# A decode attention and gMLP kernel: two rows a partition of w_out come through two GpSimd gathers instead of SyncE's queue

## The chip, the core and the metric

The kernel runs on one core of a Trainium2 chip. The metric is the device time of one execution in microseconds (us). The core has five engines that run their own instruction streams: PE (matmul, with PEld for its weight loads), DVE (vector), ACT (scalar), POOL (GpSimd) and SP (SyncE, which here only issues transfers). Sixteen DMA engines move data between HBM and the on-chip SBUF, which has 128 partitions. Transfers issued by one engine stand in a queue of their own.

## What is computed

One decode step for one token `x` of 576 values: a normalised `xn` feeds a windowed attention (32 query heads, 16 key/value heads, the last 4096 positions of the caches) and a gated MLP, and both are added to `x`. Cut to what matters:

```python
xn = layernorm(x)
# attention: W = 4096, Dh = 128, each key/value head serves two query heads
q = (xn @ wq).reshape(32, 128)
p = softmax(q @ k[:, -W:].T * 128 ** -0.5)
A = (p @ v[:, -W:]).reshape(1, 4096) @ wo            # wo: 4096 x 576
# gMLP with one token, Fh = 2304
z = gelu(xn @ w_in)                                  # w_in: 576 x 4608
g = w_sp * layernorm(z[2304:]) + b_sp
B = (z[:2304] * g) @ w_out                           # w_out: 2304 x 576
out = x + A + B
```

Some 51 MB of weights and caches are read for it, and almost nothing is written.

## The kernel before

**The stream of loads.** SP issues 17 loads, and each begins once its slot in SBUF is free. In order: wq in two parts (`rest` in slot "d", the remainder in "a"), K[0] ("b"), K[1] ("c"), w_in in two parts (seven pieces in "a", two in `rest`), K[2] ("b"), V[0] ("c"), K[3] ("d"), V[1] ("a"), V[2] ("b"), V[3] ("c"), then w_out (all NF = 18 rows a partition, L106) and wo in five pieces of 14, 9, 6, 2 and 1 rows a partition (L108 and L109). Every load covers all 128 partitions. A row of w_out or wo in one partition is 576 values of two bytes, 1152 B. Partition p of w_out holds rows 18p to 18p + 17.

**The work.** Keys come in four groups g of four heads, each group in two halves c. `keys(g, c)` transposes half a group on DVE (L258), `scores(g, c)` multiplies it with the query on PE (L265), `sm_a(g)` takes the maximum on DVE (L286 and the small steps of `spread`) and the exponentials on ACT (L292), `sm_b(g)` transposes the probabilities on DVE (L303, tile `pt`) and rearranges them on ACT (L306), `sums(g)` and `pv(g)` multiply by ones and by V on PE (L312, L329), and `tail(g)` normalises on DVE (L339, L343), turns the result by small matmuls (L350) and writes 32 partitions of `Y` (L357). The gated MLP is woven in: `z_mms` (L365), `z_exp`, `z_gelu` and `z_norm`, which ends in `hv` (128 x 18). In `z_norm` POOL does one instruction, a power (L404), between two groups of DVE's.

**The order** is written out by hand (lines 420 to 477); each engine does its instructions in the order of the program. Small results in PSUM share one buffer, the pool `ps_m` with tag "m", and `pt` is a single buffer of the pool `single`.

**The end.** `out_mms` (L463) adds one row of w_out or wo a partition to the two output accumulators: two matmuls, one over 264 and one over 312 columns, which stand in different column groups of PE and run side by side. `hv` rows 0 to 11 come first, then `tail(3)`, then `hv` rows 12 to 17, then the 32 rows of wo with `Y` as the weights, in the order of their loads. After the last, DVE and ACT copy the accumulators out (L480, L481), and ACT stores them (L482).

Of the kernel before, what the change touches and what calls it, by code (L numbers as in the profile page):

```python
# [7 lines left out]

FP32 = mybir.dt.float32
BF16 = mybir.dt.bfloat16  # L10
ALU = mybir.AluOpType
ACT = mybir.ActivationFunctionType
AXX = mybir.AxisListType.X

D = 576
# [12 lines left out]
NF = FH // 128  # L28
CUT = (0, 264, D)
XP = D // 3  # L30
EPS = 1e-5
SCALE = DH ** -0.5
GELU_C = 0.7978845608028654
# [4 lines left out]
def kernel(  # L38
# [21 lines left out]
    work = ctx.enter_context(tc.tile_pool(name="work", bufs=2))  # L60
    ktpool = ctx.enter_context(tc.tile_pool(name="ktpool", bufs=2))
    single = ctx.enter_context(tc.tile_pool(name="single", bufs=1))
    ps_s = ctx.enter_context(tc.tile_pool(name="ps_s", bufs=1, space=bass.MemoryType.PSUM))
    ps_o = ctx.enter_context(tc.tile_pool(name="ps_o", bufs=1, space=bass.MemoryType.PSUM))
    ps_m = ctx.enter_context(tc.tile_pool(name="ps_m", bufs=1, space=bass.MemoryType.PSUM))
# [8 lines left out]
    def rows(slot, src, name, lo, n, at=None):  # L74

        w = src.shape[1]
        if at is None:
            t = big.tile([P, n * w], BF16, name=f"{name}{lo}", tag=slot)[:]
        else:
            t = slot[:, at:at + n * w]  # L80
        v = t.rearrange("p (s c) -> p s c", c=w)
        nc.sync.dma_start(v, src.rearrange("(p s) c -> p s c", p=P)[:, lo:lo + n, :])  # L82
        return [(lo + s, v[:, s, :]) for s in range(n)]
# [19 lines left out]
    V[2] = load_kv("b", A_v_cache, 2, "v")  # L103
    V[3] = load_kv("c", A_v_cache, 3, "v")
    ends = [big.tile([P, TP * DH], BF16, name=f"end{n}", tag="ad"[n]) for n in range(2)]
    wout_sb = rows(ends[0], B_w_out, "wout", 0, NF, 0)  # L106
    wo_sb = []
    for n, t, at in ((14, 1, 0), (9, 1, 14), (6, 0, NF), (2, 0, NF + 6), (1, 0, NF + 8)):  # L108
        wo_sb += rows(ends[t], A_wo, "wo", len(wo_sb), n, at * D)  # L109
# [132 lines left out]
    for a in range(4):  # L242
        for h in range(2):
            for k2 in range(2):
                nc.vector.tensor_scalar_mul(qbv[:, a, h, k2], qpv[:, h, k2], mask4[:, a:a + 1])


    Y = const.tile([P, 32], BF16, name="Y")
    KT = {}
# [34 lines left out]
    def sm_a(g):  # L284
        s = S[g % 2]
        nc.vector.tensor_reduce(out=mx[:, 0:1], in_=s[:], op=ALU.max, axis=mybir.AxisListType.XY)  # L286
        bk = spread(mx, mb, g, ALU.max, "m")
        nm = work.tile([P, 1], FP32, name=f"nm{g}", tag="nm")
        nc.vector.tensor_scalar_mul(nm[:], bk[:, 0:1], -SCALE)  # L289
        for x in range(GK):  # L290
            lo, hi = 32 * x, 32 * x + 32
            nc.scalar.activation(pz[lo:hi, :, :, x, :], s[lo:hi].rearrange("p a (t r e) -> p (a t) r e", r=8, e=2),  # L292
                                 ACT.Exp, bias=nm[lo:hi, 0:1], scale=SCALE, accum_out=lx[lo:hi, g:g + 1])
        st[g] = {}
# [101 lines left out]
    def z_norm(G, sz):  # L396
        psz = ps_m.tile([P, 512], FP32, name="psz", tag="m")
        nc.tensor.matmul(psz[:, 0:2], lhsT=ones_f[:], rhs=sz[:], start=True, stop=True)
        mz = const.tile([P, 4], FP32, name="mz")
        nc.vector.tensor_scalar_mul(mz[:, 0:2], psz[:, 0:2], 1.0 / FH)  # L400
        nc.vector.tensor_mul(mz[:, 2:3], mz[:, 0:1], mz[:, 0:1])
        nc.vector.tensor_sub(mz[:, 2:3], mz[:, 1:2], mz[:, 2:3])
        nc.vector.tensor_scalar_add(mz[:, 2:3], mz[:, 2:3], EPS)  # L403
        nc.gpsimd.tensor_tensor(out=mz[:, 3:4], in0=mz[:, 2:3], in1=mhalf[:], op=ALU.pow)  # L404
        zn = const.tile([P, NF], FP32, name="zn")
        nc.vector.tensor_scalar(out=zn[:], in0=G[:, 1], scalar1=mz[:, 0:1], scalar2=mz[:, 3:4],
                                op0=ALU.subtract, op1=ALU.mult)
        nc.vector.tensor_scalar(out=zn[:], in0=zn[:], scalar1=wb[:, 0:1], scalar2=wb[:, 1:2],
                                op0=ALU.mult, op1=ALU.add)
        hv = const.tile([P, NF], BF16, name="hv")  # L410
        nc.vector.tensor_mul(hv[:], G[:, 0], zn[:])
        return hv
# [7 lines left out]
    for g in range(2):  # L420
        for c in range(2):
            keys(g, c)
            scores(g, c)
            if g == 1 and c == 0:
                sm_a(0)
    zps = z_mms()
    sm_b(0)
    sm_a(1)
# [24 lines left out]
    tail(1)  # L453
    sm_a(3)
    hv = z_norm(G, sz)
    sums(2)
    pv(2)
    tail(2)
    sm_b(3)
    sums(3)  # L460
    pv(3)

# [12 lines left out]
    out_hv(2)  # L475
    for t, wv in wo_sb:
        out_mms(Y, t, wv, t == 31)

    res = const.tile([1, D], BF16, name="res")
    nc.vector.tensor_copy(res[:, 0:CUT[1]], acc[0])  # L480
# [32 lines left out]
```

## Time and profile before

| What | Before |
|---|---|
| median of 3 runs | 126.97 us (126.78 to 127.12) |
| the profiled execution | 126.89 us |
| its span, first to last instruction | 125.1 us |
| HBM read over the span | 50.96 MB, 407 GB/s |
| busy: PE, DVE, ACT, POOL | 70.8, 78.5, 43.2, 7.1 us |

The lines cited are those of the kernel before. The profile has a record for every instruction and for every DMA packet; busy times do not count waiting. The chain of waits starts at the last instruction and goes back, at each step, to what released it. The view of stretches gives, for chosen windows of time, the busy time of each engine and the mean busy share of the 16 DMA engines. The granted clock of PE is a share of its full speed, 1.0 or 0.5.

### The profile page before, as it was taken

The page shows a single profiled execution, that of the slowest core. Times are in us where ns is not written, and L with a number is a line of the kernel's source. Part 1 is how long each engine was busy: PE and PEld are TensorE (multiplying, and loading weights), DVE is VectorE, ACT ScalarE, POOL GpSimd, SP SyncE. Part 2 cuts the span into 40 slices and gives each one's busy share as a digit, 9 for nine tenths or more (in the row PEclk, how much of TensorE's full clock was granted, in tenths as well). Part 3 has the DMA queues.
Part 4 walks back from the last instruction along what each step waited for, and adds up shares of the span by engine and source line. Part 5 has one row for each costly group of instructions (what it writes and reads, how often), then busy time and mean ns, then how long its engine had stood idle before and what let it go on. Part 6 is the DMA issues. An engine that isn't in the chain of part 4 may idle for free.

```text
span 125.1 us, 1617 instructions
## 1 busy us (share of the span) xinstructions
PE 70.8 (57%) x626; PEld 28.9 (23%) x626; DVE 78.5 (63%) x150; ACT 43.2 (34%) x101; POOL 7.1 (6%) x19
## 2 busy tenths in 40 slices
PE   0012841009878469998390992059892932049992
PEld 0001201001101013998000131002211411015850
DVE  6745025899799976308999367999938359003301
ACT  2100011000000956996069008707801941940001
POOL 2961000000000000000000000000000100000000
PEclk9999998555995867755559599657998555555899
DMA  4999899998999999898999989999999999999960
GB/s 118 511 422 440 385 471 440 398 492 356 487 420 402 385 493 461 377 492 372 461 451 398 482 367 477 401 451 430 409 482 398 451 394 440 418 413 416 428 237 0
DMA packets 2611, 51.06 MB, mean 408 GB/s; under 512 B 299, under 2 KB 428, under 8 KB 684
## 3 DMA queue, kind: packets, MB, share of 16 engines
q1 hardware_dynamic: 2592, 50.96, 95.2%
q8 instruction: 5, 0.08, 0.2%
q14 instruction: 2, 0.02, 0.0%
q10 hardware_dynamic: 12, 0.00, 0.0%
HBM read 50.96 MB, written 0.00 MB: 407 GB/s over the span
## 4 chain that ended last, share of the span: by engine, by line
DMA 61%; DVE 30%; PE 5%; SPq 1%; issue 1%; ACT 0%; DVEq 0%
DMA k<-in_A_k_cache_dram 37%; DMA end<-in_A_wo_dram 25%; DVE kT L258 22%; DVE pt L303 4%; PE S L265 3%; PE acc L465 1%; SPq L82 1%; DVE mx L286 1%; DVE on L343 1%; DVE om L339 1%; PE yps L350 0%; ACT res L481 0%; DVE rs L320 0%; DVE mt L275 0%; DVE mb L281 0%
## 5 line engine op out<-in xcount | busy, mean ns | idle before, releaser
L265 PE MATMUL S<-kT,Qb 128*8 128x512 bf16 x128 | 32.5, 1148 | 23.3 <-DVE kT L258 22.8
L258 DVE STREAM_TRANSPOSE kT<-k 128x1024 f32<-128x1024 f32 x32 | 36.8, 1207 | 6.5 <-DMA k<-in_A_k_cache_dram 6.5
L292 ACT ACTIVATE pz<-S,nm 32x1024 bf16<-32x1024 f32 x16 | 19.1, 1192 | 33.6 <-DVE nm L289 20.6
L306 ACT COPY PT<-pt 32x128 f32<-32x128 f32 x64 | 19.8, 309 | 17.2 <-DVE pt L303 16.5
L329 PE MATMUL ops<-v,PT 128*32 128x512 bf16 x128 | 11.0, 505 | 6.8 <-ACT PT L306 6.8
L265 PEld LDWEIGHTS <-Qb 128*8 128x8 bf16 x128 | 3.5, 96 | 45.0 <-issue 34.8
L303 DVE STREAM_TRANSPOSE pt<-pz 128x1024 f32<-128x1024 f32 x8 | 9.4, 1210 | 0.8 <-ACT pz L292 0.8
L339 DVE SCALAR_TENSOR_TENSOR om<-ops,rs,dmask 128x512 f32<-128x512 f32 x4 | 3.0, 750 | 10.5 <-PE ops L329 10.3
L365 PEld LDWEIGHTS <-win 128*128 128x128 bf16 x126 | 7.9, 165 | 1.9 <-issue 1.9
L365 PE MATMUL zps<-XT,win 128*128 128x2 bf16 x126 | 8.0, 202 | 0.0
L286 DVE TENSOR_REDUCE mx<-S 128x1 f32<-128x1024 f32 x4 | 4.9, 1214 | 3.9 <-PE S L265 3.9
L329 PEld LDWEIGHTS <-PT 128*32 128x32 bf16 x128 | 3.7, 117 | 11.5 <-ACT PT L306 6.9
L226 ACT CAST q_rep<-qps 128x512 bf16<-128x512 f32 x2 | 1.2, 586 | 14.9 <-DVE q_rep L228 14.9
L404 POOL TENSOR_TENSOR mz<-mz,mhalf 128x1 f32<-128x1 f32 x1 | 0.6, 554 | 85.5 <-DVE mz L403 85.5
L183 PE MATMUL ps_x<-ones_b,xtw 1*128 1x1 bf16 x9 | 0.4, 162 | 8.7 <-DVE xtw L181 8.7
L465 PE MATMUL acc<-end,Y 128*1 128x312 bf16 (+1 forms) x64 | 4.9, 285 | 0.3 <-DMA end<-in_A_wo_dram 0.3
L228 DVE CAST q_rep<-qps 128x512 bf16<-128x512 f32 x2 | 1.4, 692 | 5.1 <-PE qps L217 4.5
L481 ACT CAST res<-acc 1x312 bf16<-1x312 f32 x1 | 0.4, 411 | 11.7 <-PE acc L465 11.7
L350 PE MATMUL yps<-on,sel 128*32 128x32 f32 x32 | 2.0, 210 | 4.1 <-DVE on L343 4.1
L343 DVE TENSOR_REDUCE on<-om 128x128 f32<-128x512 f32 x4 | 4.2, 1042 | 0.1
L480 DVE CAST res<-acc 1x264 bf16<-1x264 f32 x1 | 0.4, 420 | 5.2 <-PE acc L465 5.2
L465 PE MATMUL acc<-end,hv 128*1 128x264 bf16 (+1 forms) x36 | 3.6, 360 | 0.0
(92 smaller groups left out, 56.6 us busy)
## 6 DMA issues: line engine op xcount, KB each, us to landing
k<-in_A_k_cache_dram SPq DMA_DIRECT2D x4, 4096.0 KB
v<-in_A_v_cache_dram SPq DMA_DIRECT2D x4, 4096.0 KB, 26.0
win<-in_B_w_in_dram SPq DMA_DIRECT2D x1, 4032.0 KB, 27.1
wq<-in_A_wq_dram SPq DMA_DIRECT2D x1, 3584.0 KB, 12.8
end<-in_B_w_out_dram SPq DMA_DIRECT2D x1, 2592.0 KB, 22.3
end<-in_A_wo_dram SPq DMA_DIRECT2D x1, 2016.0 KB
end<-in_A_wo_dram SPq DMA_DIRECT2D x1, 1296.0 KB
rest<-in_B_w_in_dram SPq DMA_DIRECT2D x1, 1152.0 KB
```

The source lines that it names most:

```text
L258: nc.vector.transpose(dst[:, 1024 * n:1024 * (n + 1)], src[:, 1024 * n:1024 * (n + 1)])
L265: nc.tensor.matmul(S[g % 2][32 * x:32 * x + 8, c, :], lhsT=Qb[:, GK * g + x, be].rearrange("p a h -> p (a h)"), rhs=kv[:, be // 2, be % 2, x],
L286: nc.vector.tensor_reduce(out=mx[:, 0:1], in_=s[:], op=ALU.max, axis=mybir.AxisListType.XY)
L292: nc.scalar.activation(pz[lo:hi, :, :, x, :], s[lo:hi].rearrange("p a (t r e) -> p (a t) r e", r=8, e=2), ACT.Exp, bias=nm[lo:hi, 0:1], sc ...
L303: nc.vector.transpose(dst[:, 1024 * n:1024 * (n + 1)], src[:, 1024 * n:1024 * (n + 1)])
L306: nc.scalar.copy(PT4[32 * a:32 * a + 32, :, x, :], pt[32 * x:32 * x + 32, :, 2 * a:2 * a + 2])
L329: nc.tensor.matmul(ops[32 * q:32 * q + 32, :], lhsT=d["PT"][:, t0 // 2:t0 // 2 + 2].rearrange("p t x h e -> p (t x h e)"), rhs=V[g][:, t0: ...
L339: nc.vector.scalar_tensor_tensor(out=om[:].rearrange("p c d -> p (c d)"), in0=ops[:], scalar=d["rs"][:, 0:1], in1=dmask[:].rearrange("p c ...
L343: nc.vector.reduce_sum(on[:], om[:].rearrange("p c d -> p d c"), axis=AXX)
L350: nc.tensor.matmul(yps[32 * g:32 * g + 32, :], lhsT=sel[:, dq, :], rhs=d["on"][:, 32 * dq:32 * dq + 32], start=(dq == 0), stop=(dq == 3), ...
L365: nc.tensor.matmul(zps[:, :, t], lhsT=wt[:, t, :], rhs=XT[:, s, :], start=(s == 0 and t == 0), stop=(s == NS - 1 and t == NF - 1), skip_gr ...
L465: nc.tensor.matmul(acc[n], lhsT=lhs[:, col:col + 1], rhs=wv[:, CUT[n]:CUT[n + 1]], start=False, stop=last, tile_position=(0, 32 * n))
```

## The change

The last two rows a partition of w_out (rows 16 and 17 of 18; 2304 B a partition, 288 KB in all) leave SP's load, which now brings `NM` = 16 rows. They come by two gathers on POOL's own queue. Gather 0 writes partition p's own pair of rows into `ext[:, 0]`, but not for 32 "spared" partitions (20 to 27, 52 to 59, 68 to 71, 88 to 91, 100 to 103, 120 to 123). Gather 1 brings those 32 pairs into 32 other, "given" partitions (72 to 87 and 104 to 119) of `ext[:, 1]`. A partition that a gather skips has an index beyond the bound. `ext` is zeroed first, so that skipped partitions add nothing.

The indices are made on the chip: POOL writes them in a row, spreads them over a diagonal, and two PE matmuls with ones turn them into a column, which DVE copies to integers. `hv`'s last two columns are moved from the spared to the given partitions by one matmul with `move`, a permuted identity. `gap.tile` is only room left empty; `ext`, `move`, `idx` and `hx` lie behind all the buffers that were there before. `both` takes turns with `pt` in its buffer.

```diff
+NX = 2
+NM = NF - NX
+PAIRS = NF // NX
+FAR = 4096
+SPARED = ((20, 8), (52, 8), (68, 4), (88, 4), (100, 4), (120, 4))
+GIVEN = (72, 80, 104, 108, 112, 116)
...
-    wout_sb = rows(ends[0], B_w_out, "wout", 0, NF, 0)
+    wout_sb = rows(ends[0], B_w_out, "wout", 0, NM, 0)
...
+    gap.tile([P, 176], BF16, name="unused")
+    ext = far.tile([P, 2, NX, D], BF16, name="ext")
+    nc.gpsimd.memset(ext[:], 0.0)
+    move = more.tile([P, P], BF16, name="move")
+    nc.gpsimd.memset(move[:], 0.0)
+    for (lo, n), at in zip(SPARED, GIVEN):
+        nc.gpsimd.tensor_copy(move[:, at:at + n], ident[:, lo:lo + n])
+    both = single.tile([P, 4, P], FP32, name="both", tag="pt")
+    which = []
+    for g in range(2):
+        col = both[:, 2 * g].bitcast(I32)
+        if g == 0:
+            nc.gpsimd.iota(col, pattern=[[PAIRS, P]], base=PAIRS - 1, channel_multiplier=0)
+            for lo, n in SPARED:
+                nc.gpsimd.memset(col[:, lo:lo + n], FAR)
+        else:
+            nc.gpsimd.memset(col, FAR)
+            for (lo, n), at in zip(SPARED, GIVEN):
+                nc.gpsimd.iota(col[:, at:at + n], pattern=[[PAIRS, n]], base=PAIRS * lo + PAIRS - 1, channel_multiplier=0)
+        diag = both[:, 2 * g + 1]
+        nc.gpsimd.tensor_copy(diag, col)
+        nc.gpsimd.tensor_tensor(out=diag, in0=diag, in1=ident[:], op=ALU.mult)
+        which.append(diag)
+
+    def rows_to_take():
+        pick = ps_m.tile([P, 2], FP32, name="pick", tag="m")
+        for g, diag in enumerate(which):
+            nc.tensor.matmul(pick[:, g:g + 1], lhsT=diag, rhs=ones_f[:, 0:1], start=True, stop=True)
+        idx = more.tile([P, 2], I32, name="idx")
+        nc.vector.tensor_copy(idx[:], pick[:])
+        which[:] = [idx[:, g:g + 1] for g in range(2)]
+
+    def load_ext():
+        pairs = B_w_out.rearrange("(r s) c -> r (s c)", s=NX)
+        for g in range(2):
+            nc.gpsimd.indirect_dma_start(
+                out=ext[:, g].rearrange("p s c -> p (s c)"), out_offset=None, in_=pairs,
+                in_offset=bass.IndirectOffsetOnAxis(ap=which[g], axis=0),
+                bounds_check=P * PAIRS - 1, oob_is_err=False)
...
             if g == 1 and c == 0:
                 sm_a(0)
+                rows_to_take()
...
     hv = z_norm(G, sz)
+    load_ext()
     sums(2)
     pv(2)
     tail(2)
     sm_b(3)
+    hx_ps = ps_m.tile([P, 32], FP32, name="hx_ps", tag="m")
+    nc.tensor.matmul(hx_ps[:, 0:NX], lhsT=move[:], rhs=hv[:, NM:NF], start=True, stop=True)
+    hx = more.tile([P, NX], BF16, name="hx")
+    nc.vector.tensor_copy(hx[:], hx_ps[:, 0:NX])
     sums(3)
     pv(3)
...
     for t, wv in wo_sb:
         out_mms(Y, t, wv, t == 31)
+        if t == 13:
+            for j in range(NX):
+                out_mms(hv, NM + j, ext[:, 0, j, :], False)
+                out_mms(hx, j, ext[:, 1, j, :], False)
```

More of the change, by code (lines that the diff above doesn't have):

```diff
@@ L10 @@
 BF16 = mybir.dt.bfloat16
+I32 = mybir.dt.int32
 ALU = mybir.AluOpType
@@ L62 @@
     single = ctx.enter_context(tc.tile_pool(name="single", bufs=1))
+    gap = ctx.enter_context(tc.tile_pool(name="gap", bufs=1))
+    far = ctx.enter_context(tc.tile_pool(name="far", bufs=1))
+    more = ctx.enter_context(tc.tile_pool(name="more", bufs=1))
     ps_s = ctx.enter_context(tc.tile_pool(name="ps_s", bufs=1, space=bass.MemoryType.PSUM))
```

## The prediction

> **What bounds the kernel now.** I read the page first, for the load of the engines.
>
> ```profile
> span 125.1 us, 1617 instructions
> ...
> DMA  4999899998999999898999989999999999999960
> ...
> q1 hardware_dynamic: 2592, 50.96, 95.2%
> q8 instruction: 5, 0.08, 0.2%
> ```
>
> The DMA engines are full from the first slice to the 38th; no compute engine is busy over 63%. So the stream of loads sets the pace, and q8, which is no load of the program, takes five turns of 16 KB on the same engines. Then the end of the chain of waits (start us, us, what):
>
> ```profile
> 90.41 30.86 DMA end<-in_A_wo_dram
> 121.27 0.04 issue
> 121.31 1.39 PE acc L465 x17
> 122.70 0.02 issue
> 122.72 0.41 ACT res L481
> ```
>
> The wo piece of 6 rows, issued at 90.41, lands at 121.27, and PE had waited 0.28 us for it. The list of DMA issues gives the last row (issued 91.35) 31.0 us to landing: 122.35. Next the view of stretches over those last microseconds (the DMA share is the column before the last):
>
> ```profile
> 120.00:120.25 0.25, 0.25 (x8) 0.15 (x6) 0.00 (x0) 0.00 (x0) 0.00 (x0) 1.00 0.91 346
> 120.25:120.50 0.25, 0.25 (x6) 0.15 (x5) 0.00 (x0) 0.00 (x0) 0.00 (x0) 1.00 0.60 230
> 121.00:121.25 0.25, 0.03 (x1) 0.00 (x0) 0.00 (x0) 0.00 (x0) 0.00 (x0) 1.00 0.23 92
> 121.25:121.50 0.25, 0.19 (x4) 0.16 (x5) 0.00 (x0) 0.00 (x0) 0.00 (x0) 1.00 0.25 92
> 121.50:121.75 0.25, 0.25 (x8) 0.24 (x6) 0.00 (x0) 0.00 (x0) 0.00 (x0) 1.00 0.27 97
> ```
>
> A share of 0.25 is four of sixteen engines: most are done by 120.5, four work on until 121.9. The 16 KB turns would explain four: windows around 36.5, 57.2, 77.7 and 101.0 us each hold one q8 packet (0.93 to 0.96 us long), and the fifth, at 120.6, comes when most engines are done. Last, the timeline, for what stands beside these:
>
> ```profile
> 56.69 3.50 DVE L258 STREAM_TRANSPOSE kT<-k 128x1024 f32<-128x1024 f32 x3 [5.44 <-DMA k<-in_A_k_cache_dram]
> 100.80 0.75 DVE L339 SCALAR_TENSOR_TENSOR om<-ops,rs,dmask 128x512 f32<-128x512 f32 x1 [1.94 <-PE ops L329]
> 117.30 0.20 DVE L357 CAST Y<-yps 32x32 bf16<-32x32 f32 x1 [0.78 <-PE yps L350]
> 117.77 3.26 PE L465 MATMUL acc<-end,Y 128*1 128x264 bf16 x44
> 121.31 0.90 PEld L465 LDWEIGHTS <-Y 128*1 128x1 bf16 x16 [0.62 <-issue]
> 122.38 0.08 PEld L465 LDWEIGHTS <-Y 128*1 128x1 bf16 x1 [0.17 <-issue]
> ```
>
> PE can start wo only when `Y` is there (117.50), and runs almost without a pause from then on; at the end it waits for the 6-row piece (0.28) and for the last row (landed 122.35, weights at 122.38). **Two things end nearly together: the late four engines and PE's own stream of rows.** The gain is capped by the second.
>
> **The loads' end.** The late engines take the last 3 rows (each engine 8 partitions, 3 x 8 x 1152 B = 27.6 KB) between the landings at 121.27 and 122.35, 1.08 us, or 25.6 KB a us. Two rows less on each are 18.4 KB, 0.72 us: the last row lands at 121.63, the 6-row piece at 120.55. The given engines get 18.4 KB more; if they are of those done by 120.5, they end 0.72 later, about 121.2. The bytes in all stay; how a gather spreads its rows over engines no row shows. It lies between all of the 0.72 taken off the late four, nothing (rows spread evenly), and 0.72 added to one of them. I take the first.
>
> [...]
>
> **PE's stream.** Removed: hv rows 16 and 17 ahead of wo (4 matmuls). Added after wo's 14th row: 4 rows (8 matmuls). The 44 matmuls from 117.77 are 22 rows; the starts of those with 312 columns, the longer of each pair, lie 0.1325 apart. Before, that stream was still at hv when Y came, and took its first wo row at 117.82; with two rows (0.27) less ahead, it takes it at 117.56. Then 32 + 4 = 36 rows: the last starts at 117.56 + 35 x 0.1325 = 122.20, and ends 0.29 later, 122.49. Before, the last started at 122.38. So PE gains 0.18, and by its times (6-row piece at 121.14, last row at 122.20) the loads above are early enough. Had the loads not moved, PE would wait as before, and the gain were 0.
>
> **The indices.** POOL's 26 small instructions follow L200 (11.1 us). Rows: a memset of 128x4096 took 3.5 us, so ext's 128x2304 some 2.0; small copies 0.2, memsets 0.1; iotas and the mask multiply have no row, between 0.1 and 0.6 (the power). Sum 6 to 10 us, done by 22; POOL is next wanted at 97.2 and the diagonals at 42. DVE's query work beside it may lose its 0.4 us of slack before K[0] (23.63); the 5.44 us at 56.69 cover that.
>
> The wait they add: DVE's index copy stands between sm_a(0) and keys(1, 1), and needs two PE matmuls that stand behind scores(1, 0). DVE would have begun keys(1, 1) at 40.20. scores(1, 0) ends at 42.16 (38.14 + 4.02), one 128x128 f32 matmul (L312) takes 0.38 to 0.55, two 0.8 to 1.1, the copy 0.2: keys(1, 1) begins at 43.1 to 43.5, 2.9 to 3.3 late. Queued behind: scores(1, 1), sm_b(0), z_mms, sm_a(1). DVE then stands ready near 54.3 and still waits for K[2] at 56.66: 2.4 of the 5.44 are left. ACT's second exponentials end near 60.5; the transposes that want them begin at 61.2. z_mms end at 62.0 to 62.4 instead of 59.03, and SP waits for them to issue K[3] and V[1]. The queue ahead of K[3] is 26.8 MB; at 430 GB/s from 1.73 it runs dry near 64. An issue took 1.0 us to its first packet (0.73 to 1.73). Room: 0.6 to 1.0. Price 0; uncovered, the stream stops for what is missing.
>
> **The rest.** Two gathers on POOL after L404 (97.7) replace nothing on SP, whose w_out load is the same one instruction with fewer bytes; `ext` is first read at 119.4, 21 us later. hx: one matmul and one copy behind sm_b(3), before sums(3); both lie in the 4.8 us in which PE waits for ACT (pv(3) at 111.04). Price 0. Outside the span lie 126.89 - 125.1 = 1.8 us; no row bears on a change there: 0.
>
> Sum, against the profiled 126.89: -0.18, 126.71; that execution stands 0.08 under the median, so **126.79** in its terms. About 0.3% (0.38 us) can be told from no change, so this counts as none.
>
> **Rivals.**
>
> 1. *PE keeps up, the loads alone set the end.* The last 16 weight loads go in 0.90 us, 0.1125 a row. At that step 36 rows take 4.05 us from 117.55, and the end follows the landing: -0.72, 126.25. Against: the 312-column starts at 0.1325, steady over 22 rows.
>
> 2. *Other engines are late than the spared.* The 16 KB turns come one engine at a time, and no view says which; the changed program has other instructions. If none of the four is relieved, but no late one given more: 0. If a late one is among the given: it ends 0.72 later, last row at 123.07, 127.69. For the forecast speaks a match of counts alone: four are spared, four are late.
>
> 3. *The other side: the gathers hold DVE.* They start at 97.7, together with z_norm's end on DVE (L406, L408, L411, then the reciprocal for tail(2)). If POOL's descriptor work shuts DVE out, these wait, then `om` (100.80), `Y`, pt, ACT's 5.0 us, pv(3) and the last Y, one for one. Slack is the 1.94 us ahead of `om`. No row shows a gather: two lie between 2 x 0.1 and 2 x 3.5 us (POOL's shortest and longest). It is slower by over 0.3% from a hold of 2.5 us (1.94 + 0.18 + 0.38); at 3.5, one longest instruction, +1.38 gives 128.35. Against: beside pz's memset on POOL (4.71 to 8.22), DVE's memset of S took 0.91 as without.
>  [...]
>
> 4. *K[3] late.* With an issue latency of 2.5 us instead of 1.0, a hole of 0.5 to 0.9: the loads end at 122.1 to 122.5, 126.8 to 127.1.
>
> **Chances.** Forecast 0.47 (own range 126.5 to 127.1; 0.40 of it within 0.3%, 0.05 faster, 0.02 slower); rival 1 0.18 (faster); rival 2 0.16 (0.13 slower, 0.03 same); rival 3 0.13 (slower); rival 4 and what else is unseen 0.06 (0.04 slower, 0.02 same). Faster 0.23, same 0.45, slower 0.32. The range reaches from rival 1 to the worse half of rival 2, 126.2 to 127.8, and leaves out most of rival 3.
>
> **What would show it.** In the changed profile: the DMA share near the end falls from 0.9 to 0 within about 1 us, without a shelf at 0.25; PE's last 36 rows run without a wait, their first at 117.5, and end near 122.5; DVE stands about 3 us before L258 near 40 and still waits over 2 us for K[2]; no dip of the DMA share at 64; `om` for group 2 at 100.8. A shelf that is still there, or longer, is rival 2; om late, rival 3; a dip, rival 4. I am wrong if the first Y row is not at 117.5, for then the cap is not where I put it.

## The result, and the profile after

The changed kernel takes 128.12 us (median of 6 runs, 127.93 to 128.41) against 126.91 (126.78 to 127.12, 6 runs) for the kernel before: a ratio of 1.0096, 95% interval 1.008 to 1.0112. It is slower by 1.2 us, and it lies outside the range that was forecast. The profiled execution took 128.41 us with a span of 126.3; before, 126.89 and 125.1. So 1.2 us of the loss lie in the span and 0.3 outside it in that pair of executions.

Lines below are those of the changed kernel: L285 and L287 are the index matmuls and their copy, L293 the gathers, L308 the transposes of the keys, L389 `om`, L521 the output rows. First the head of its page, with its DMA row (busy share of the 16 engines in 40 slices) and its queues:

```profile
span 126.3 us, 1670 instructions
...
DMA  3999999899998999999899998989989899999940
...
q1 hardware_dynamic: 2592, 50.66, 94.0%
q0 software_dynamic: 160, 0.30, 0.6%
q8 instruction: 5, 0.08, 0.2%
```

The loads still fill the span to the 38th slice, and part of the 39th. The gathers are the 160 packets of q0, with 0.3 MB and 0.6% of the engines' time, and as many bytes less are in q1. The end of the chain of waits (start us, us, what):

```profile
90.95 32.16 DMA end<-in_A_wo_dram
123.15 0.68 PE acc L521 x6
123.85 0.41 ACT res L541
```

The chain still ends in a wo piece, but it is now the piece of 2 rows, landed at 123.11, and six matmuls of three rows follow it; before it was the piece of 6 rows, landed at 121.27, with seventeen. The timeline says which waits PE has among the last rows (the number in brackets is the idle time ahead, and what ended it):

```profile
116.26 0.20 DVE L407 CAST Y<-yps 32x32 bf16<-32x32 f32 x1 [0.53 <-PE yps L400]
...
119.42 1.36 PE L521 MATMUL acc<-end,Y 128*1 128x264 bf16 x18 [0.36 <-DMA end<-in_A_wo_dram]
...
121.47 0.96 PE L521 MATMUL acc<-end,Y 128*1 128x264 bf16 x12 [0.69 <-DMA end<-in_A_wo_dram]
...
123.15 0.66 PE L521 MATMUL acc<-end,Y 128*1 128x264 bf16 x6 [0.72 <-DMA end<-in_A_wo_dram]
```

The last part of `Y` is written 1.04 us earlier than before (117.30), and PE waits for loads three times, 1.77 us together. PE has time to spare; the loads do not come. The view of stretches (us, busy time by engine, then granted clock, DMA share, GB/s) shows how the loads end:

```profile
120.75:121.00 0.25, 0.03 (x1) 0.00 (x0) 0.00 (x0) 0.00 (x0) 0.00 (x0) 1.00 1.06 374
121.00:121.25 0.25, 0.00 (x0) 0.00 (x0) 0.00 (x0) 0.00 (x0) 0.00 (x0) 1.00 0.67 254
121.75:122.00 0.25, 0.25 (x8) 0.25 (x5) 0.00 (x0) 0.00 (x0) 0.00 (x0) 1.00 0.25 74
122.25:122.50 0.25, 0.18 (x3) 0.00 (x0) 0.00 (x0) 0.00 (x0) 0.00 (x0) 1.00 0.06 9
122.75:123.00 0.25, 0.00 (x0) 0.00 (x0) 0.00 (x0) 0.00 (x0) 0.00 (x0) 1.00 0.08 28
```

Nearly all engines work until 121.0, as the rebalancing wanted; before, the share was down to 0.6 by 120.5. The share then falls, and from 122.25 to 123.04 it is a shelf of 0.06 to 0.08. That is one engine of sixteen. The last row lands at 123.47 on it, and on the next engine at 122.52. The fifth 16 KB packet of q8 started at 120.90 and took 0.93 us.

The second thing to see is the index wait and what it moves (timeline):

```profile
42.38 0.61 PE L285 MATMUL pick<-ones_f,both 128*128 128x1 f32 x4
...
43.02 0.16 DVE L287 CAST idx<-pick 128x2 int32<-128x2 f32 x1 [2.64 <-PE pick L285]
43.09 4.62 DVE L308 STREAM_TRANSPOSE kT<-k 128x1024 f32<-128x1024 f32 x4
...
56.51 4.63 DVE L308 STREAM_TRANSPOSE kT<-k 128x1024 f32<-128x1024 f32 x4 [2.19 <-DMA k<-in_A_k_cache_dram]
...
62.14 0.54 SPq L98 DMA_DIRECT2D k<-in_A_k_cache_dram  x1
```

DVE stands 2.64 us for the index and begins `keys(1, 1)` at 43.09 instead of 40.20; it has 2.19 of its 5.44 us before K[2] left, and K[3] is issued at 62.14 instead of 59.06. Summed over all engines, the bytes moved by a given time fall behind those of before by 0.10 us at 64, 0.23 at 68, 0.50 at 102 and 0.70 at 110. The loss is not spread evenly, as the packets show below.

### The profile page after: what moved, and what is told of

It is laid out like the page before. It is cut to its first block, busy times and chain, and to the rows that moved or that the text cites. A ratio compares the mean times of both kernels' runs of the same rounds, so it can differ in the third digit from the quotient of the medians.

```text
span 126.3 us, 1670 instructions
## 1 busy us (share of the span) xinstructions
PE 70.7 (56%) x635; PEld 29.5 (23%) x635; DVE 80.4 (64%) x152; ACT 43.4 (34%) x101; POOL 14.8 (12%) x47
## 4 chain that ended last, share of the span: by engine, by line
DMA 48%; DVE 37%; PE 8%; ACT 1%; issue 1%; SPq 1%; ACTq 1%; POOL 0%; DVEq 0%
DMA end<-in_A_wo_dram 25%; DVE kT L308 21%; DMA k<-in_A_k_cache_dram 18%; DMA xrow<-in_A_x_dram 5%; DVE pt L353 4%; PE S L315 3%; PE qps L227 3%; DVE Qb L255 2%; DVE xn L212 2%; DVE q_rep L238 1%; DVE xtw L191 1%; DVE mx L336 1%; ACT q_rep L236 1%; SPq L92 1%; DVE on L393 1%
## 5 line engine op out<-in xcount | busy, mean ns | idle before, releaser
L315 PE MATMUL S<-kT,Qb 128*8 128x512 bf16 x128 | 33.0, 1162 | 21.1 <-DVE kT L308 20.6
L308 DVE STREAM_TRANSPOSE kT<-k 128x1024 f32<-128x1024 f32 x32 | 36.8, 1207 | 2.3 <-DMA k<-in_A_k_cache_dram 2.2
L379 PE MATMUL ops<-v,PT 128*32 128x512 bf16 x128 | 10.5, 487 | 4.2 <-ACT PT L356 4.2
L389 DVE SCALAR_TENSOR_TENSOR om<-ops,rs,dmask 128x512 f32<-128x512 f32 x4 | 3.0, 750 | 9.1 <-PE ops L379 8.9
L521 PE MATMUL acc<-end,Y 128*1 128x264 bf16 (+1 forms) x64 | 5.0, 285 | 1.8 <-DMA end<-in_A_wo_dram 1.8
L362 PE MATMUL lps<-lx,lsum 128*128 128x1 f32 x8 | 1.9, 304 | 4.6 <-DVE hx L515 2.5
L521 PEld LDWEIGHTS <-Y 128*1 128x1 bf16 x64 | 3.4, 83 | 3.4 <-issue 2.9
```

Source lines behind the costliest of these rows:

```text
L308: nc.vector.transpose(dst[:, 1024 * n:1024 * (n + 1)], src[:, 1024 * n:1024 * (n + 1)])
L315: nc.tensor.matmul(S[g % 2][32 * x:32 * x + 8, c, :], lhsT=Qb[:, GK * g + x, be].rearrange("p a h -> p (a h)"), rhs=kv[:, be // 2, be % 2, x],
L379: nc.tensor.matmul(ops[32 * q:32 * q + 32, :], lhsT=d["PT"][:, t0 // 2:t0 // 2 + 2].rearrange("p t x h e -> p (t x h e)"), rhs=V[g][:, t0: ...
L389: nc.vector.scalar_tensor_tensor(out=om[:].rearrange("p c d -> p (c d)"), in0=ops[:], scalar=d["rs"][:, 0:1], in1=dmask[:].rearrange("p c ...
L521: nc.tensor.matmul(acc[n], lhsT=lhs[:, col:col + 1], rhs=wv[:, CUT[n]:CUT[n + 1]], start=False, stop=last, tile_position=(0, 32 * n))
```

## The experiments

The table holds the result in short, and the sections behind it tell each step. Down to e14 each kernel has one edit more than the line above it; e17 relieves 16 partitions more and also spreads the given rows over other partitions. The difference is the ratio less one, times 126.9.

| Kernel | median us | ratio to before, 95% interval | difference us |
|---|---|---|---|
| the changed kernel | 128.12 | 1.0096, 1.008 to 1.0112 | +1.2 |
| index copy later on DVE (e1) | 127.86 | 1.0075, 1.0058 to 1.0092 | +0.95 |
| and fewer instructions on POOL (e13) | 127.71 | 1.0065, 1.0049 to 1.008 | +0.8 |
| and the pairs to other partitions (e14) | 126.88 | 1.0004, 0.9995 to 1.0013 | +0.05 |
| and 16 partitions more relieved (e17) | 126.74 | 0.9986, 0.9977 to 0.9995 | -0.2 |

### The index wait, and the gathers by themselves

Four kernels: the copy of the index moved behind `keys(1, 1)` on DVE, ahead of `z_mms` (e1); the indices but no gathers, with 18 rows of w_out from SP again (e2); one gather in which every partition gets its own pair, with no partition spared (e3); and products of w_out left out (e4, below).

```diff
 e1:
-                rows_to_take()
+                pick = rows_to_take()
+    rows_as_index(pick)
 e2:
-    wout_sb = rows(ends[0], B_w_out, "wout", 0, NM, 0)
+    wout_sb = rows(ends[0], B_w_out, "wout", 0, NF, 0)
-    load_ext()
-        for t, wv in wout_sb[6 * c:6 * c + 6]:
+        for t, wv in wout_sb[6 * c:min(6 * c + 6, NM)]:
-                out_mms(hv, NM + j, ext[:, 0, j, :], False)
+                out_mms(hv, NM + j, wout_sb[NM + j][1], False)
 e3:
-            for lo, n in SPARED:
-                nc.gpsimd.memset(col[:, lo:lo + n], FAR)
-        for g in range(2):
+        for g in range(1):
             nc.gpsimd.indirect_dma_start(
```

> The index copy on DVE moves behind keys(1, 1), so DVE no longer waits 2.64 us for PE; all else as in the changed kernel (128.1 us). Theory hole (the late issue of K[3] at 62.1 us opened a gap in the stream at 64 us and left the engines out of step, so 32 KB packets took 1230 ns instead of 1213 from 62 to 102 us): K[3] is issued near 59.1 again, packets are back at 1213 ns, the loads end 0.3 to 0.4 us earlier, 127.7 us. Theory gathers (their own packets cost the stream what it lost): no change, 128.1. Theory fetch (the fifth 16 KB instruction fetch at 120.9 us makes one loaded engine 0.95 us late): no change, 128.1.

> The changed kernel with all of its index work, but without the gathers: SP loads all 18 rows of w_out again, PE multiplies the same number of rows in the same order. Theory gathers: the stream is as before the change but for the hole, the loads end near 122.3 as before, 126.9 to 127.2 us. Theory hole: 0.35 us of the lost 0.7 stays, 127.2 to 127.5. Theory fetch: PE's program is as long as in the changed kernel, so the fifth fetch comes near 120.9; it costs 0.95 us if it falls on an engine that is still loaded (about 127.9) and nothing if the engine is done.

> One gather of all 128 partitions' own two rows, none skipped, none moved to another partition (the second half of ext stays zero and is multiplied all the same). So the gather is there and the rebalancing is not. If sparing four engines brings their 0.72 us: without it the four that served a 16 KB fetch end 1.4 us behind the rest again, and the last of them, with the fifth fetch or not, sets the end: 128.1 to 128.8 us. If the skipped indices of the second gather cost (its packets of 8 bytes): 127.9. Theory fetch alone: 128.1.

Measured: e1 127.86 (ratio 1.0075, 1.0058 to 1.0092), e2 127.83 (1.0065, 1.0044 to 1.0087), e3 127.43 (1.0039, 1.0025 to 1.0053). In e1 `keys(1, 1)` starts at 40.23 and K[3] is on time again; the bytes are 0.04 us behind at 68 and 0.15 at 110, not 0.23 and 0.70. In e2, which has no gather at all, they are 0.32 behind at 68 and 0.41 at 110, and one engine lands its last row at 123.20. So the loss of the stream comes mostly from the index wait, not from the gathers. e3 came out under all its forecasts (127.9 to 128.8).

The packets show how the wait costs. The profile does not number the engines, but a packet starts within a few ns of where the last one of its engine ends, and every engine carries the loads in the same order of sizes, so the packets can be joined into sixteen chains (worked out from the packets' records; in places where two engines end within a few ns the joining is a choice, and it is led by those sizes). Before, every engine goes over to K[3] without a pause, at 64.1 to 66.0. In e2 K[3] is issued at 61.90, and fourteen engines still go over without a pause; two stand empty for 0.8 us each, and their first packets of K[3] start at 65.39 and 66.09 and take 1.85 and 2.06 us in place of 1.21. The second of these two is the engine that lands last, and the fifth 16 KB packet is not in its chain. So e2's 127.83 lies near the 127.9 that the fifth packet was to give, but by luck. The chain of waits has its 6-row piece 0.8 us later than before:

```profile
90.40 31.68 DMA end<-in_A_wo_dram
122.07 0.04 issue
122.12 1.45 PE acc L520 x18
```

In e3 two engines stand empty, for 1.9 and 0.6 us, and the first of them lands last; and in the changed kernel one, for 0.8: it is the one that lands next to last, at 122.52. With the late copy (e1, and e5 and e6 below) none does.

Two kernels more have both edits: late copy without gathers (e5), and late copy with one plain gather (e6).

> The index work without the gathers, and with the index copy behind keys(1, 1): SP loads all 18 rows, K[3] is issued near 59.1 us. Against the run with the index work alone (127.83 us) this differs only in where DVE waits. Theory hole: all of what that run lost comes from the late K[3], so this one is as fast as the kernel before, 126.9 us, four engines ending near 122.3. Rival (POOL's index work, the stalled DVE instruction near 12 us or the longer PE program cost something themselves): 127.4 or more.

> One gather of all partitions' own two rows, index copy behind keys(1, 1): a gather, no rebalancing, no hole. If the gather as such costs the stream 0.1 us: loads end at 122.4 on the four engines that served a 16 KB fetch, 127.0 us. The difference to the rebalanced kernel with the late copy (15 engines done by 121.65) is what sparing those four brings at the loads' end: 0.7 us by the prediction. Rival, that gathers cost the 0.7 us which the stream lost: 127.6.

Measured: e5 127.09 (1.0024, 1.0015 to 1.0034), with the span of before (125.0); e6 126.94 (1.0007, 0.9997 to 1.0017). So e5 lies between its two forecasts: what is left, about 0.27 us, lies outside the span and is told below. By e2 and e5 the index wait costs 0.5 us (by the ratios) to 0.7 (by the medians) where nothing is rebalanced, and e2's executions spread from 127.19 to 128.12; by the changed kernel and e1 it costs 0.26 there, where another engine ends behind the one that stood empty. A gather of all 128 pairs in e6 costs nothing that can be told from before. And e1, which differs from e6 in the spared and given partitions (and in eight records on POOL, of which more below), loses 0.92 to it: moving these rows to these engines is what costs.

How it costs is in e1's stretches and timeline:

```profile
121.00:121.25 0.25, 0.25 (x9) 0.25 (x6) 0.00 (x0) 0.00 (x0) 0.00 (x0) 1.00 0.44 157
121.25:121.50 0.25, 0.25 (x9) 0.19 (x6) 0.00 (x0) 0.00 (x0) 0.00 (x0) 1.00 0.03 9
121.75:122.00 0.25, 0.12 (x1) 0.00 (x0) 0.00 (x0) 0.00 (x0) 0.00 (x0) 1.00 0.03 5
122.00:122.25 0.25, 0.00 (x0) 0.00 (x0) 0.00 (x0) 0.00 (x0) 0.00 (x0) 1.00 0.07 9
```

```profile
120.65 1.23 PE L525 MATMUL acc<-end,Y 128*1 128x264 bf16 x16 [0.28 <-DMA end<-in_A_wo_dram]
...
123.02 0.30 PE L525 MATMUL acc<-end,Y 128*1 128x264 bf16 x2 [1.14 <-DMA end<-in_A_wo_dram]
```

The share falls from 0.44 to 0.03 within a quarter of a microsecond: fifteen engines land their last row between 120.64 and 121.65, just as the rebalancing was to do. The sixteenth lands it at 122.97, and PE stands 1.14 us for it with one row to go. Its packets show why. The fifth 16 KB packet runs from 120.96 to 121.89; then, and only then, come three rows of 1152 B that were left, until 122.26. The chains also show which engine it is: it carries eight packets of gathered rows, where an engine that is neither spared nor given carries four, so it is one of the four given ones. In the changed kernel the fifth 16 KB packet is on a given engine too, the one that lands at 123.47. And four engines carry only the short packets of skipped pairs; they are those that had the 16 KB packets at 37.6, 57.3, 76.5 and 100.8. So the four spared were the four late ones.

### Moving the fifth 16 KB packet

If that packet sits at a fixed place of PE's instructions, fewer instructions ahead of it move it past the end. The products of the first 9 rows of w_out (e4) or of 15 of them (e7, with the late copy) are left out for that.

```diff
-        for t, wv in wout_sb[6 * c:6 * c + 6]:
+        for t, wv in wout_sb[max(9, 6 * c):6 * c + 6]:
```

> The changed kernel without the products of w_out's first nine rows a partition (18 matmuls of PE, which waits for loads at that time anyway), so that PE's program is 36 instructions shorter ahead of the last rows; all loads are there. Theory fetch: PE reaches the 16 KB boundary only when the last rows have landed, the fifth fetch comes after 122 us, no engine stands 0.95 us behind, the last row lands near 122.5 instead of 123.47, 127.2 us. Theories hole and gathers: no change, 128.1.

> The changed kernel with the index copy behind keys(1, 1) and without the products of w_out's first 15 rows a partition (30 matmuls), so that PE's program is 60 instructions shorter ahead of the last rows. Theory fetch: the fifth 16 KB fetch comes after 121.5 us or not at all, no engine stands behind, the last row lands at 121.65 instead of 122.97; PE is free earlier and follows the loads: 126.4 to 126.7 us, faster than the kernel before. If the one late engine has another cause: 127.8 as with the late copy alone.

Measured: e4 128.32 (1.0127, 1.0094 to 1.0159), a miss: with 36 instructions fewer the packet came at 121.73, before the last landing at 123.23. But it is not what made e4 slow. The engine that lands last does not have the packet in its chain; it stood empty for 1.7 us at 65 (another one for 1.6), since e4 still has the index wait, and the packet fell on an engine whose last row was through. So e4 says nothing on the price of the packet. e7 128.33 (1.0149, 1.0085 to 1.0213), with executions of 127.01, 127.77, 128.89 and 129.56, too far apart for a verdict and all above the forecast. In the profiled execution of e7, the one of 127.01, the packet came at 126.21, after everything, and all sixteen engines land their last row by 121.73: 0.6 us earlier than before, and 1.24 earlier than in e1. That is what the rebalancing is worth without the packet, seen once. The end did not follow in full, since PE ran the first rows of wo slowly (26 weight loads, 13 rows, in 2.70 us from 116.31; the last 34, 17 rows, in 2.46) and ended at 122.5; and the other executions of e7 were slower, for a reason that no profile of them shows.

e11 goes the other way: 80 more instructions of PE (the small matmul for `hx` written 41 times), on top of e10, which is told below.

> As e10_few_pool, with the small matmul for hx written 41 times in place of once, in the time in which PE waits for ACT (80 instructions of PE more, the same result): the fifth 16 KB fetch, which stands at a fixed place in PE's instructions, comes some 20 rows of wo earlier, near 117.8 us, while every DMA engine is loaded, the one that serves it being one of those neither spared nor given (they have 0.9 us to spare at the end). Theory (a fetch costs its engine 0.93 us, and hurts by what that engine still has to do): the last row lands by 121.7 in every run, PE ends near 122.3, 126.1 to 126.4 us, and the runs lie within 0.3 of one another. If the engine that serves it is one of those given rows: last landing 122.5, 127 us. Rival (the end is bound by PE's own stream, whatever the fetch does): as e10_few_pool.

Measured: 127.02 (1.0015, 1.0006 to 1.0024). A miss: the packet still came at 120.44, with 47 of PE's recorded instructions to go, where it is 39 or 40 in most other kernels (also in e4, with 36 instructions fewer), but 26 in e1, 42 in e14, 44 in e3 and 52 in e2. So it does not stand at a fixed count from the beginning, nor quite at one from the end. What sets its moment is open. The profile of e11 shows a second way in which it hurts: all loads' packets were through by 121.38, but one engine's note of completion, 4 bytes behind the 16 KB packet, took effect at 122.46, where the others took 0.3 us (q1 holds 288 packets of 4 bytes, sixteen for each of SP's 18 loads).

### Which partitions are given the pairs

Two kernels give the pairs to other partitions, both with the late copy: 0 to 15 and 32 to 47 (e8), and eight blocks of four at 16, 28, 48, 60, 64, 92, 96 and 124 (e9).

```diff
 e8:
-GIVEN = (72, 80, 104, 108, 112, 116)
+GIVEN = (0, 32, 8, 12, 40, 44)
 e9:
-SPARED = ((20, 8), (52, 8), (68, 4), (88, 4), (100, 4), (120, 4))
-GIVEN = (72, 80, 104, 108, 112, 116)
+SPARED = ((20, 4), (24, 4), (52, 4), (56, 4), (68, 4), (88, 4), (100, 4), (120, 4))
+GIVEN = (16, 48, 28, 60, 64, 96, 92, 124)
```

> The changed kernel with the index copy behind keys(1, 1), and the 32 pairs go to partitions 0 to 15 and 32 to 47 instead of 72 to 87 and 104 to 119; the same 32 partitions are spared. Theory given (the engine of the fifth fetch is one of those that got more load, done by 120.4 us before and loaded until 121.3 now): that engine is relieved, the fifth fetch finds it done, and the last row lands near 121.7 instead of 122.97; PE's rows then end near 122.3 and the time is 126.6 to 126.8 us. Theory any (the fetch hits a loaded engine whichever partitions are given): 127.8 as with the late copy alone.

> As the run before, but the pairs go to partitions 16 to 19, 28 to 31, 48 to 51, 60 to 67, 92 to 99 and 124 to 127. Theory given: again 126.6 to 126.8 us, since the engine of the fifth fetch is not among these either; if only one of the two is that fast, that engine belongs to the partitions of the other. Theory any: 127.8.

Measured: e8 127.17 (1.0024, 1.0012 to 1.0037), e9 127.50 (1.0063, 1.0044 to 1.0081), with 126.76 as its lowest: both above the forecast of 126.6 to 126.8, so the placing alone does not pay. In e8's profile the fifth packet came early, at 120.17, and found an engine that was neither spared nor given with its last rows still to move; it landed them last, at 122.26. So the moment of the packet counts beside the placing. In e9's profile the loads are done by 121.58 and PE at 121.92, each some 0.75 us before the kernel before. But POOL's next to last drain starts 0.43 us behind the instruction ahead of it, where it is 0.03 in the others, so that the span, 125.0, hardly shows a gain. That gap led to the next pair.

### What lies outside the span

Counted with those of its sequencer, POOL has 35 records in the profile before and 65 after. The time outside the span was 1.8 us in the profiled executions with up to 57 POOL records, 2.0 to 2.1 with 61 or 65, and with 71 (e9) it was 1.8 again, with the gap inside the span. e10 is e9 with the same work in 56 POOL records; e12 is the kernel before with 30 tiny memsets on POOL and nothing else.

```diff
 e10: two blocks 32 partitions apart in one instruction, both diagonals at once
+TURNS = ((20, 16), (24, 28), (68, 64), (88, 92))
+    two = lambda t, lo, n: t[:, lo - lo % 64:lo - lo % 64 + 64].rearrange("p (a b) -> p a b", b=32)[:, :, lo % 64:lo % 64 + n]
+    for lo, at in TURNS:
+        nc.gpsimd.tensor_copy(two(move, at, 4), two(ident, lo, 4))
...
+    nc.gpsimd.tensor_copy(both[:, 1:4:2], both[:, 0:4:2].bitcast(I32))
 e12:
+    for _ in range(30):
+        nc.gpsimd.memset(junk[:], 0.0)
```

> As e9_give_mixed, but POOL's preparation is written in fewer instructions (two blocks of partitions 32 apart in one; both diagonals in one copy and one multiply): POOL's rows in the profile fall from 71 to about 56. Nothing else is changed. Theory: what is left over outside the stream of loads is a fetch of POOL's own instructions at the program's end, which comes once POOL's instructions pass a block. In the profiles so far the time outside the span is 1.78 to 1.79 us with 35 or 57 POOL rows, 2.00 to 2.14 with 61 or 65, and with 71 rows 1.79 again but a gap of 0.43 us ahead of POOL's next to last drain inside the span. Expected by it: that gap is 0.03 us, the time outside the span 1.8, and every run some 0.3 to 0.4 below e9_give_mixed (127.50 median, 126.76 lowest): median 127.1, lowest 126.4. Rival (the gap comes from the gathers or from the end of the loads): gap and times as in e9_give_mixed.

> The kernel before, with 30 memsets of a small unused tile on POOL more, at about 20 us: 65 POOL rows in the profile, as in the changed kernel, and no index, no gather, no other change. Theory (POOL's instructions past a block are fetched at the program's end): span 125.1 as before, 2.0 to 2.1 us outside it in place of 1.8, 127.1 to 127.2 us. Rival (the time outside the span comes from the gathers' queue or its descriptors): 126.9, as before.

Measured: e12 127.04 (1.0012, 1.0002 to 1.0021). Its eleven spans lie at 124.8 to 125.2, as before, and 1.92 to 2.13 us lie outside (mean 2.01), against 1.75 to 1.90 in the 27 runs of the kernel before beside it (mean 1.82). So 30 instructions on POOL that nothing waits for cost 0.19 us outside the span. e10 126.92 (1.0002, 0.9987 to 1.0018): the gap is 0.03 and 1.8 to 1.9 us lie outside. Both about as expected, though e10's median and e12's lie a little under the forecast. In the profiles of e12 and of the changed kernel an 8 KB instruction packet follows the end of the span by 1.8 us; that it is POOL's fits these counts, but no record names it, and e2 and e5, with 61 records and 2.1 us outside, show no such packet. That POOL's instructions cost the time is shown; by what means is not.

### The same with few POOL instructions: which engine is hit

With both side costs out, three placings, each with 32 pairs moved: to the partitions of the change (e13), to those of e8 (e14), or four partitions at a time to 0 to 19, 28 to 31, 64 to 67 and 92 to 95 (e15). The packets show what the first two do: four engines carry twice the gathered packets, eight in place of four. That e15's pairs fall to eight engines, with half of the 0.72 us for each, was the author's assumption; no view shows it.

```diff
 e13:
+TURNS = ((20, 72), (24, 76), (68, 80), (88, 84))
 e14:
+TURNS = ((20, 0), (24, 4), (68, 8), (88, 12))
 e15, with the distance of the two given blocks:
+TURNS = ((20, 0, 4), (24, 8, 4), (68, 16, 12), (88, 64, 28))
```

> As e10_few_pool (late index copy, POOL's preparation in 56 rows), but the pairs go to partitions 72 to 87 and 104 to 119 again, as in the changed kernel. Theory A (it matters which engines are given rows: the one that serves the fifth 16 KB fetch is among those given): one engine lands the last row near 122.9, alone, and the time is that of e1_late_copy less what POOL's end costs, 127.86 - 0.2 = 127.6 to 127.7. Theory B (the fifth fetch hits any engine that is still loaded, whichever was given): 126.9 to 127.3 as e10_few_pool, with runs as far apart.

> The same with the pairs given to partitions 0 to 15 and 32 to 47, as in e8_give_low. Theory A: 127.17 - 0.2 = 126.9 to 127.0, runs within 0.5 of one another. Theory B: as e13_few_high.

> [...] If the engine of the fifth fetch is not among the eight, or has only 0.36 more: last row by 121.7 alone and 126.3 to 126.6 us, the version that beats both. If the fetch hits a loaded engine all the same: last landing 122.0 to 122.5 and 126.8 to 127.0. PE's own stream would end near 122.2 in either case.

Measured: e13 127.71 (1.0065, 1.0049 to 1.008), e14 126.88 (1.0004, 0.9995 to 1.0013), e15 126.91 (1.0002, 0.999 to 1.0013). Theory A holds, with its numbers: the same kernel, 0.83 us apart by which partitions get the pairs. The ends of the two chains of waits, e13 first:

```profile
91.59 31.45 DMA end<-in_A_wo_dram
123.08 0.32 PE acc L525 x2
123.43 0.41 ACT res L545
```

```profile
114.31 2.14 PE acc L525 x18
116.61 5.74 PE acc L525 x77
122.37 0.41 ACT res L545
```

In e13 one engine lands its last row at 123.04, the next at 121.85, and PE ends with two matmuls behind that landing. In e14 all land by 121.98, and the chain goes through 77 matmuls without a load in it: PE's own stream sets the end. The chains agree: in e13 the fifth packet (120.86) is on the given engine that lands last, and in e14 (120.46) on one that is neither spared nor given, just as its last row is through. The engine of the fifth packet is thus one of those that the change gives rows to.

e15 did not pay in the median: 126.33 in the profiled execution, with all loads in by 121.68, but nine of eleven runs above 126.8. The last step is to relieve that engine too: 48 partitions are spared, the 32 and also 72 to 87, half of those that e13 gives pairs to. It was assumed, and no view shows, that this takes the same from each of the four engines that e13 loads, half of the 0.72 us.

```diff
 source, blocks, their distance, length; target, distance
+TURNS = ((20, 2, 32, 8, 32, 12), (72, 1, 0, 16, 0, 16), (68, 2, 32, 4, 64, 28), (88, 2, 32, 4, 28, 32))
```

> [...] Given: 0 to 15, 32 to 39, 44 to 51, 64 to 67, 92 to 95, 28 to 31 and 60 to 63. POOL rows about 57. Theory (what is left in most runs of e14 and e15 is that the fetch still catches the end of that engine, as in the profile of e11, where its last note of completion waited for it and came at 122.46): with 0.36 us less to move that engine is done by 120.1, ahead of the fetch at 120.45, all land by 121.7, and 126.2 to 126.5 us with runs within 0.4 of one another. Rival (PE's stream or its clock sets the rest): 126.9, runs as far apart as in e15_few_spread.

> As e16_spare_more was meant: in that one the block of 72 to 87 went to partitions 16 to 31 in place of 0 to 15, of which 20 to 27 belong to relieved engines and 28 to 31 were given twice, so that four rows' pairs were left out. Now it goes to 0 to 15 and all pairs are there. Theory as there: the engine of the fifth fetch is done before the fetch, all land by 121.7, 126.2 to 126.5 us. e16_spare_more, with two engines less relieved than meant, gave 126.68 against 126.83 of the kernel before, so at most 126.68. Rival (PE's stream or its clock sets the rest): 126.7 to 126.9.

Measured: e16, which leaves the pairs of partitions 84 to 87 out, 126.68 (0.9987, 0.9977 to 0.9998); e17 126.74 (0.9986, 0.9977 to 0.9995), its runs between 126.58 and 126.87. e17's page and the end of its chain:

```profile
span 124.8 us, 1662 instructions
```

```profile
91.00 29.86 DMA end<-in_A_wo_dram
120.90 1.41 PE acc L530 x17
122.33 0.41 ACT res L550
```

e17 computes all that the kernel before does and beats both kernels: 126.74 against 126.92 beside it. The 6-row piece lands 0.4 us earlier than before, the last row at 121.94 instead of 122.34, and the spread of the runs, 0.29 us, is a quarter of e10's 1.11. The gain is under the forecast of 126.2 to 126.5: after the 6-row piece PE still has 17 matmuls (1.41 us) to do, and one engine lands at 121.94, not 121.7. In its profile the fifth packet, at 120.16, falls on an engine whose last row is through at that moment, and the engine that lands last, one of those that are given the most rows, does not have it in its chain; so there the packet holds nothing any more. The other executions left no profile.

## Why the prediction was wrong, by its own steps

**What bounds the kernel: right, and it held the answer.** The stream sets the end, and four engines were late by their turns of 16 KB. It also said of the fifth turn that "the fifth, at 120.6, comes when most engines are done". In the changed kernel no engine is through before 120.77 and no given one before 121.76. That sentence was not carried over to the kernel after.

**The loads' end: the step that failed.** Of the given engines it said "if they are of those done by 120.5, they end 0.72 later, about 121.2", and it took the first of its three values, all of the 0.72 gained. That this comes off the late four needs the 32 spared partitions to be theirs, which no run before showed; e1's packets show it, with four engines that carry only short gathered packets and that had the 16 KB packets before the fifth. The relieved engines did what was said: in e1 all of them land by 121.65, against a forecast of 121.63. Three given ones did as well. The fourth also had the fifth packet to carry. Before, that packet began at 120.62, and no engine with rows left has it in its chain (the four late engines land within 0.3 us of one another), so it cost nothing; an engine given 18.4 KB more had to do both. e13 and e14 show it by the placing alone, 0.83 us. The rebalancing was costed by bytes per engine, with the fifth packet left where it cost nothing.

**Rival 2 was right in its size and its form, not in its reason.** "If a late one is among the given: it ends 0.72 later, last row at 123.07, 127.69": e13 has 123.04 and 127.71. But the engine was not late before; it became late by the change. The rival had 0.13 for this side.

**PE's stream: wrong, and harmless here.** I had said I would be wrong if the first `Y` row was not at 117.5. `Y` was written by 116.46 and its rows ran from 116.51, 1.04 us earlier, since `om` of group 2 came 0.40 earlier (100.40), ACT's copies of `PT` 0.59, and PE's granted clock was full from 114 on in the stretches (1.00), and not from 117 on (before, 0.50 up to 116 and 0.76 in the next us). The cap of 0.18 was not there; PE waits 1.77 us for loads. Where `Y` came late, in e14 (117.22), the forecast's picture returns: 77 matmuls without a wait, the last row at 122.0.

**The indices: the times right or near, the price wrong.** Forecast were a delay of 2.9 to 3.3 us (2.89), 2.4 us left before K[2] (2.19) and K[3] issued at 62.0 to 62.4 (62.14). The room of "0.6 to 1.0" was not there on every engine. It counted 1.0 us from an issue to its first packet, read at the start of the kernel, where the queue was empty. K[3], issued at 62.14, has its first packet on one engine only at 65.98, 3.84 us later, and that engine stood empty for 0.83 us; in e2 and e3 the last one starts 4.19 and 4.28 us after the issue. Over all engines the stream loses 0.13 us between 64 and 68, and more after that, up to 0.5 at 102. In part this is a size of its own: between 66 and 102, the mean time of a 32 KB packet in stretches of 4 us is 1.213 us before in all but two, and 1.216 to 1.232 after. What the wait is worth: 0.26 us here (e1), 0.5 to 0.7 in e2. Rival 4 had the place, a hole of 0.5 to 0.9 us and 0 to 0.3 for the price. The hole came, on single engines; what the rival did not have is that such an engine does not catch up and can land last.

**The rest: the gathers at 0 right, outside the span 0 wrong.** A plain gather costs nothing that can be told (e6). Outside the span lie 0.2 us more, from POOL's number of instructions and not from its gathers (0.19 in e12, which has none; e13 against e1: 0.15 in the median).

**Rival 3 did not come.** The timeline beside the gathers (POOL's issue of each, DVE's work between and after them):

```profile
97.71 0.29 DVE L456 TENSOR_SCALAR zn<-G,mz 128x18 f32<-128x18 f32 x1 [0.68 <-POOL mz L454]
...
97.99 1.26 POOL L293 DMA_INDIRECT ext<-in_B_w_out_dram,idx  x1 [0.32 <-issue]
98.04 0.29 DVE L458 TENSOR_SCALAR zn<-zn,wb 128x18 f32<-128x18 f32 x1
...
99.56 1.00 POOL L293 DMA_INDIRECT ext<-in_B_w_out_dram,idx  x1 [0.31 <-issue]
...
100.40 0.75 DVE L389 SCALAR_TENSOR_TENSOR om<-ops,rs,dmask 128x512 f32<-128x512 f32 x1 [1.59 <-PE ops L379]
```

L458 runs inside the first gather's issue and takes 0.29 us, as L456 just ahead of it. `om` is earlier than before. But DVE was slow beside POOL at another place, which the prediction had priced as "its 0.4 us of slack" only:

```profile
11.94 2.01 POOL L260 MEMSET ext<- 128x2304 bf16 x1
12.01 2.10 DVE L212 TENSOR_SCALAR xn<-x_col,mv 128x9 f32<-128x9 f32 x1 [0.70 <-POOL mv L210]
```

Before, the same instruction took 0.29 us:

```profile
11.69 0.29 DVE L202 TENSOR_SCALAR xn<-x_col,mv 128x9 f32<-128x9 f32 x1 [0.68 <-POOL mv L200]
```

The 2.10 us end at 14.11, 0.16 us after POOL's memset (13.95); what links the two no record shows. It costs nothing in the end, since DVE still waits for K[2] at 56.5 (e5's span is that of before).

**What it sums to.** Index wait 0.26, POOL's instructions 0.15 to 0.2, the placing 0.83: 1.24 to 1.29 of the measured 1.2. These are the steps from the changed kernel to e14, so they have to add up to the difference between the two; what they show beside it is that e14, with all three out, is level with the kernel before, and that the forecast gain of 0.18 is not there either. Rival 2's 127.69 lay inside the range of 126.2 to 127.8. What carried the time out of it are the two terms that stood in the sum at 0, the index wait and the time outside the span.

## What to carry to other kernels

Before work is moved to an engine that is idle at the end, ask what lands on that engine in the time that it will now be busy; here it was a packet that costs 0.93 us and that came, in the kernel before, when its engine was done. Cost a rebalancing with every load that an engine has, the program's own instructions among them, and try the placing two ways before the idea is judged. A wait that moves the issue of one load by 3 us is to be priced by the engine that gets its first packet last, and not by the mean queue that is left and an issue time read from an empty one (1.0 us there, up to 4.3 on one engine here).

## What was not expected of the hardware

- Instructions come in packets of 16 KB on the DMA engines that also carry the loads, 0.88 to 0.96 us each, five times. No record says whose they are; that they are PE's is an estimate from the counts (1,252 instructions on PE before, at most 150 on any other engine). PE's waits among the last rows of the changed kernel (0.36, 0.69 and 0.72 us) all end with a load, none with such a packet; but a load that shares the engine does wait: in e1 its last packet ends at 122.26, and the next engine's at 121.35.
- A 16 KB packet can also hold back the 4 byte note of completion of a load whose data are through (e11: it took effect at 122.46, for packets that ended at 121.38).
- 30 memsets on POOL that nothing waits for cost 0.19 us outside the span (e12).
- On one engine the first packet of a load came 3.8 us after its issue, with the queue ahead just running empty, and 1.0 us after it at the start (the changed kernel's K[3]; the first load before).
- A gather of pairs on POOL's queue took 1.26 and 1.00 us to issue and some 10 us to land in a stream that was full: 107.25 for the first, issued at 97.99.
- DVE's subtract and multiply over 128x9 took 2.10 us in place of 0.29 beside a memset of POOL.
